# A Strassen stage with 16-bit sums and a weight scale made on chip

The Strassen-like stage of a transformer layer formed its weight and activation sums in 32 bits (the type float32r). The change forms them in float16, after scaling the weights by a power of two that the kernel takes from their L1 norm (the sum of their absolute values), and scales the results back.

## The chip, the cores and the metric

Each run uses one core of a Trainium2 chip (trn2). The metric is the device time of one execution in microseconds (us); each kernel was run several times, beside runs of the kernel before on the same chip. The experiments went in three batches, on different chips; the kernel before took 803.37, 803.18 and 803.22 us there (medians), so times are compared across batches. "Clock" is the mean granted TensorE clock of a run, 1.0 being full speed. All runs told of here were fast (within 1.5% of the fastest of their kernel). Engines: PE is TensorE's matmuls, PEld its weight loads, DVE VectorE, ACT ScalarE, POOL GpSimd.

## The reference

```python
x = A_x                                       # 2048 x 1024, bf16
h = x + attention(layernorm(x), wqkv, wo)     # 32 heads, 8 dilated keys per position
y = layernorm(h)
out = h + ((y @ w_gate) * (y @ w_up)) @ w_down   # w_gate, w_up: 1024 x 3584
```

## The kernel before

The 2048 rows go in four chunks of 512. Chunks 0 and 1 take the gate and up matmuls plainly (`ffn1`). Chunks 2 and 3 are taken together: with weights cut into halves and the two chunks as the other pair of halves, seven half-size products stand for eight (a Strassen form). There are 14 blocks (`pair_block`), each of 7 products x 4 matmuls x 2 (gate, up) = 56 matmuls of 512 columns. The weight sums are made by GpSimd, the activation sums once by VectorE. Line numbers in profiles of other kernels differ: L622 (matmul of a product) is L653 in the changed one.

```python
    def ffn1(c, lnT):
        hT = []
        for b in range(7):
            if b == 5 and c + 1 < NCH:
                hss[c + 1] = load_x(c + 1, "h", nc.sync)
            for j in range(4):
                pg = psum.tile([128, TC], F32, tag="mm", name=f"pg{c}_{b}_{j}")
                mm_group(pg, wts["wg", c, b], j, lnT)
                gs = t1k.tile([128, TC], BF, tag="t1k", name=f"gs{c}_{b}_{j}")
                nc.scalar.copy(gs[:], pg[:])
                bg.step(GROUP_US)
                pu = psum.tile([128, TC], F32, tag="mm", name=f"pu{c}_{b}_{j}")
                mm_group(pu, wts["wu", c, b], j, lnT)
                us = t1k.tile([128, TC], BF, tag="t1k", name=f"us{c}_{b}_{j}")
                nc.scalar.copy(us[:], pu[:])
                nc.vector.tensor_tensor(gs[:], gs[:], us[:], ALU.mult)
                bg.spend(0.45)
                bg.step(GROUP_US)
                hT.append(gs)
            retire(2)
        return hT

    ...
    def weight_sums(n, i):
        wt = pair["w", n]
        a11, a12 = wt[:, 0:4, i, 0:128], wt[:, 4:8, i, 0:128]
        a21, a22 = wt[:, 0:4, i, 128:256], wt[:, 4:8, i, 128:256]
        sw = wpool.tile([128, 4, 4, 128], F32R, tag="w", name=f"sw_{n}_{i}")
        nc.gpsimd.tensor_tensor(sw[:, 0], a21, a22, ALU.add)
        nc.gpsimd.tensor_tensor(sw[:, 1], sw[:, 0], a11, ALU.subtract)
        nc.gpsimd.tensor_tensor(sw[:, 2], a11, a21, ALU.subtract)
        nc.gpsimd.tensor_tensor(sw[:, 3], a12, sw[:, 1], ALU.subtract)
        pair["s", n, i] = sw
        state["live"] += 1

    def activation_sums(l2, l3):
        b11, b12, b21, b22 = l2[:, 0:4, :], l3[:, 0:4, :], l2[:, 4:8, :], l3[:, 4:8, :]
        t1 = att.tile([128, 4, TC], F32R, tag="kD", name="t1p")
        t2 = att.tile([128, 4, TC], F32R, tag="vD", name="t2p")
        t3 = att.tile([128, 4, TC], F32R, tag="prod", name="t3p")

        t4 = lnTp.tile([128, 4, TC], F16, tag="lnT", name="t4p")
        bc = att.tile([128, 4, TC], F32R, tag="oD", name="bcp")
        nc.scalar.copy(bc[:], b22)
        nc.vector.tensor_tensor(t1[:], b12, b11, ALU.subtract)
        nc.vector.tensor_tensor(t2[:], b22, t1[:], ALU.subtract)
        nc.vector.tensor_tensor(t3[:], b22, b12, ALU.subtract)
        nc.vector.tensor_tensor(t4[:], b21, t2[:], ALU.subtract)
        pair["b"] = (b11, b21, t1, t2, t3, t4, bc)

    def product(ps, lhs, rhs, fresh):
        for ko in range(4):
            nc.tensor.matmul(ps[:], lhsT=lhs[:, ko, :], rhs=rhs[:, ko, :], start=(fresh and ko == 0),
                             stop=(ko == 3), skip_group_check=not fresh)

    def pair_block(n, hts):
        b11, b21, t1, t2, t3, t4, bc = pair["b"]
        wt = pair["w", n]
        gu = range(2)
        sw = [pair["s", n, i] for i in gu]
        out = [hts, [t1k.tile([128, TC], BF, tag="t1k", name=f"up{n}_{k}")[:] for k in range(4)]]

        def bank(k, i):
            return psum.tile([128, TC], F32, tag="mm", name=f"p{k}{n}_{i}")

        xb, yb, zb, vb, p5 = [[None] * 2 for _ in range(5)]
        for i in gu:
            xb[i] = bank("x", i)
            product(xb[i], wt[:, 0:4, i, 0:128], b11, True)
            yb[i] = bank("y", i)
            nc.scalar.copy(yb[i][:], xb[i][:])
        for i in gu:
            vb[i] = bank("v", i)
            product(vb[i], sw[i][:, 0], t1, True)
            p5[i] = att.tile([128, TC], F32, tag=("lg", "t3")[i], name=f"p5{n}_{i}")
            nc.scalar.copy(p5[i][:], vb[i][:])
            product(yb[i], sw[i][:, 1], t2, False)
            zb[i] = bank("z", i)
            nc.scalar.copy(zb[i][:], yb[i][:])
        for i in gu:
            product(zb[i], sw[i][:, 2], t3, False)
            nc.vector.tensor_tensor(out[i][3], zb[i][:], p5[i][:], ALU.add)
            product(xb[i], wt[:, 4:8, i, 0:128], b21, False)
            nc.scalar.copy(out[i][0], xb[i][:])
        for i in gu:
            product(zb[i], wt[:, 4:8, i, 128:256], t4, False)
            nc.scalar.copy(out[i][2], zb[i][:])
            product(yb[i], sw[i][:, 3], bc, False)
            nc.vector.tensor_tensor(out[i][1], yb[i][:], p5[i][:], ALU.add)
        for k in (3, 0, 2, 1):
            nc.vector.tensor_tensor(out[0][k], out[0][k], out[1][k], ALU.mult)
        state["live"] -= 3

    ...
    hT = ffn1(1, lnT2)            # then, in order:
    bg.finish(atts[2])
    l2, hs2 = wo_ln2(2)           # output projection of chunk 2, layernorm
    ffn2(1, 0, hT, hs)
    bg.finish(atts[3])
    l3, hs3 = wo_ln2(3)
    activation_sums(l2, l3)
    load_pair(0); load_pair(1)
    weight_sums(0, 0)
    ffn2(1, 1, hT, hs, {0: lambda: weight_sums(0, 1)})
    ...                           # h23: where the products of gate and up go
    for n in range(NP):           # NP = 14
        if n + 1 < NP:
            weight_sums(n + 1, 0)
            weight_sums(n + 1, 1)
            if n + 2 < NP:
                load_pair(n + 2)
        ...
        pair_block(n, h23[4 * n:4 * n + 4])
    ...                           # ffn2 of chunks 2 and 3
```

`bg.step` puts pieces of the attention of later chunks, nearly all of it VectorE work, between the matmul groups.

Of the kernel before, what the change touches and what calls it, by code (L numbers as in the profile page):

```python
# [7 lines left out]

BF = mybir.dt.bfloat16
F32 = mybir.dt.float32  # L10
F32R = mybir.dt.float32r
F16 = mybir.dt.float16
ALU = mybir.AluOpType
ACTF = mybir.ActivationFunctionType
# [4 lines left out]
D = 1024  # L19
# [6 lines left out]
TC = 512  # L26
NCH = S // TC
SUB = TC // 4
KO = D // 128
# [49 lines left out]
def kernel(  # L79
# [11 lines left out]
    nc = tc.nc  # L91
# [6 lines left out]
    const = ctx.enter_context(tc.tile_pool(name="const", bufs=1))  # L98
    wpool = ctx.enter_context(tc.tile_pool(name="wstream", bufs=7))
    lnTp = ctx.enter_context(tc.tile_pool(name="lnT", bufs=3))  # L100
    lnp = ctx.enter_context(tc.tile_pool(name="ln", bufs=4))
    hp = ctx.enter_context(tc.tile_pool(name="hp", bufs=8))
    t1k = ctx.enter_context(tc.tile_pool(name="t1k", bufs=30))
    small = ctx.enter_context(tc.tile_pool(name="small", bufs=4))
    att = ctx.enter_context(tc.tile_pool(name="att", bufs=1))
    psum = ctx.enter_context(tc.tile_pool(name="psum", bufs=8, space=PSUM))
# [48 lines left out]
    wts = {}  # L155
    state = {"next": 0, "live": 0, "limit": 1}
# [343 lines left out]
    def wo_ln2(c):  # L500
# [25 lines left out]
        retire(2)  # L526
        return lnT, hs

    def ffn1(c, lnT):
        hT = []  # L530
        for b in range(7):
# [10 lines that stand above are left out]
                us = t1k.tile([128, TC], BF, tag="t1k", name=f"us{c}_{b}_{j}")  # L542
                nc.scalar.copy(us[:], pu[:])  # L543
                nc.vector.tensor_tensor(gs[:], gs[:], us[:], ALU.mult)
                bg.spend(0.45)
                bg.step(GROUP_US)
                hT.append(gs)
            retire(2)
        return hT
# [6 lines left out]
    def ffn2(c, hf, hT, hs, between={}):  # L556
        if c == NCH - 1 and hf == 1:
            for t, lo, n in ((0, 0, 512), (1, 0, 512), (2, 0, 512), (3, 0, 256), (3, 256, 256)):
                acc = psum.tile([128, n], F32, tag="mm", name=f"accl{t}_{lo}")
                for f in range(NF):  # L560
                    nc.tensor.matmul(acc[:], lhsT=hT[f][:, bass.ts(t, 128)],  # L561
                                     rhs=wts["wd", c, hf, f // 7][:, f % 7, bass.ds(lo, n)],
                                     start=(f == 0), stop=(f == NF - 1))
                ffn2_store(c, t, hf, acc, hs, lo, n)
            return
        acc = [psum.tile([128, 512], F32, tag="mm", name=f"acc{c}_{hf}_{t}") for t in range(4)]
        for b in range(4):
            for j in range(7):
                f = b * 7 + j
                for t in range(4):  # L570
                    nc.tensor.matmul(acc[t][:], lhsT=hT[f][:, bass.ts(t, 128)],  # L571
                                     rhs=wts["wd", c, hf, b][:, j, :],
                                     start=(f == 0), stop=(f == NF - 1))
                bg.step(0.86)
            retire()
            if b in between:
                between[b]()
        for t in range(4):
            ffn2_store(c, t, hf, acc[t], hs)
            bg.spend(0.7)  # L580
# [3 lines left out]
    pair = {}  # L584
# [5 lines left out]
        pair["w", n] = wt  # L590
        state["live"] += 1

    def weight_sums(n, i):
        wt = pair["w", n]
        a11, a12 = wt[:, 0:4, i, 0:128], wt[:, 4:8, i, 0:128]
        a21, a22 = wt[:, 0:4, i, 128:256], wt[:, 4:8, i, 128:256]
        sw = wpool.tile([128, 4, 4, 128], F32R, tag="w", name=f"sw_{n}_{i}")
        nc.gpsimd.tensor_tensor(sw[:, 0], a21, a22, ALU.add)  # L598
        nc.gpsimd.tensor_tensor(sw[:, 1], sw[:, 0], a11, ALU.subtract)
        nc.gpsimd.tensor_tensor(sw[:, 2], a11, a21, ALU.subtract)  # L600
        nc.gpsimd.tensor_tensor(sw[:, 3], a12, sw[:, 1], ALU.subtract)
        pair["s", n, i] = sw
        state["live"] += 1

    def activation_sums(l2, l3):
        b11, b12, b21, b22 = l2[:, 0:4, :], l3[:, 0:4, :], l2[:, 4:8, :], l3[:, 4:8, :]
        t1 = att.tile([128, 4, TC], F32R, tag="kD", name="t1p")
        t2 = att.tile([128, 4, TC], F32R, tag="vD", name="t2p")
        t3 = att.tile([128, 4, TC], F32R, tag="prod", name="t3p")

        t4 = lnTp.tile([128, 4, TC], F16, tag="lnT", name="t4p")
        bc = att.tile([128, 4, TC], F32R, tag="oD", name="bcp")
        nc.scalar.copy(bc[:], b22)
        nc.vector.tensor_tensor(t1[:], b12, b11, ALU.subtract)
        nc.vector.tensor_tensor(t2[:], b22, t1[:], ALU.subtract)
        nc.vector.tensor_tensor(t3[:], b22, b12, ALU.subtract)
        nc.vector.tensor_tensor(t4[:], b21, t2[:], ALU.subtract)
        pair["b"] = (b11, b21, t1, t2, t3, t4, bc)

    def product(ps, lhs, rhs, fresh):  # L620
        for ko in range(4):
            nc.tensor.matmul(ps[:], lhsT=lhs[:, ko, :], rhs=rhs[:, ko, :], start=(fresh and ko == 0),  # L622
                             stop=(ko == 3), skip_group_check=not fresh)

    def pair_block(n, hts):
        b11, b21, t1, t2, t3, t4, bc = pair["b"]
        wt = pair["w", n]
        gu = range(2)
        sw = [pair["s", n, i] for i in gu]
        out = [hts, [t1k.tile([128, TC], BF, tag="t1k", name=f"up{n}_{k}")[:] for k in range(4)]]  # L630

        def bank(k, i):
# [7 lines that stand above are left out]
            nc.scalar.copy(yb[i][:], xb[i][:])  # L640
        for i in gu:
            vb[i] = bank("v", i)
            product(vb[i], sw[i][:, 0], t1, True)
            p5[i] = att.tile([128, TC], F32, tag=("lg", "t3")[i], name=f"p5{n}_{i}")
            nc.scalar.copy(p5[i][:], vb[i][:])
            product(yb[i], sw[i][:, 1], t2, False)
            zb[i] = bank("z", i)
            nc.scalar.copy(zb[i][:], yb[i][:])
        for i in gu:
            product(zb[i], sw[i][:, 2], t3, False)  # L650
            nc.vector.tensor_tensor(out[i][3], zb[i][:], p5[i][:], ALU.add)
            product(xb[i], wt[:, 4:8, i, 0:128], b21, False)
            nc.scalar.copy(out[i][0], xb[i][:])  # L653
        for i in gu:
            product(zb[i], wt[:, 4:8, i, 128:256], t4, False)
            nc.scalar.copy(out[i][2], zb[i][:])
            product(yb[i], sw[i][:, 3], bc, False)
            nc.vector.tensor_tensor(out[i][1], yb[i][:], p5[i][:], ALU.add)
        for k in (3, 0, 2, 1):
            nc.vector.tensor_tensor(out[0][k], out[0][k], out[1][k], ALU.mult)  # L660
        state["live"] -= 3

    atts = {}

# [30 lines left out]
    lnT2, hs = nxt  # L695
# [4 lines left out]
        ffn2(0, hf, hT, hs)  # L700
    lnT2, hs = nxt
    hT = ffn1(1, lnT2)
    bg.finish(atts[2])
    l2, hs2 = wo_ln2(2)
    h3 = att.tile([128, 4, D], BF, tag="qD", name="h3")
# [5 lines left out]
    activation_sums(l2, l3)  # L711
    load_pair(0)
    load_pair(1)
    weight_sums(0, 0)
    ffn2(1, 1, hT, hs, {0: lambda: weight_sums(0, 1)})

    h23 = [t1k.tile([128, TC], BF, tag="t1k", name=f"hq{i}")[:] for i in range(24)]
    for i in range(4):
        ht = hp.tile([128, D], BF, tag="h", name=f"hq_h{i}")
        h23 += [ht[:, 0:TC], ht[:, TC:2 * TC]]  # L720
    for ht in (att.tile([128, KO, TC], BF, tag="oT", name="hq_o"),
               l3):
        h23 += [ht[:, k, :] for k in range(KO)]
    for i in range(4):
        ht = lnp.tile([128, D], BF, tag="ln", name=f"hq_n{i}")
        h23 += [ht[:, 0:TC], ht[:, TC:2 * TC]]
    for n in range(NP):
        if n + 1 < NP:
            weight_sums(n + 1, 0)
            weight_sums(n + 1, 1)  # L730
            if n + 2 < NP:
                load_pair(n + 2)
        else:
            state["limit"] = len(stream)
            pump()
        pair_block(n, h23[4 * n:4 * n + 4])
# [35 lines left out]
```

## Time and profile before

| | before |
|---|---|
| time, median of the first 3 runs | 803.0 us (802.61 to 803.44) |
| span of the profiled run | 801.5 us |
| start of output projection, chunk 1 | 288.56 us |
| first Strassen block | 523.39 us |
| end of the 14th block | 701.45 us, so 12.72 us each |
| TensorE busy / VectorE / ScalarE / GpSimd | 99 / 70 / 30 / 21% of the span |

Read it from TensorE: it is busy from its first microseconds to the end, so the sum of its instruction spacings is the time. The other engines matter only when they make it wait. The lines are in the prediction below.

### The profile page before, as it was taken

The page shows a single profiled execution, that of the slowest core. Times are in us where ns is not written, and L with a number is a line of the kernel's source. Part 1 is how long each engine was busy: PE and PEld are TensorE (multiplying, and loading weights), DVE is VectorE, ACT ScalarE, POOL GpSimd, SP SyncE. Part 2 cuts the span into 40 slices and gives each one's busy share as a digit, 9 for nine tenths or more (in the row PEclk, how much of TensorE's full clock was granted, in tenths as well). Part 3 has the DMA queues.
Part 4 walks back from the last instruction along what each step waited for, and adds up shares of the span by engine and source line. Part 5 has one row for each costly group of instructions (what it writes and reads, how often), then busy time and mean ns, then how long its engine had stood idle before and what let it go on. Part 6 is the DMA issues. An engine that isn't in the chain of part 4 may idle for free.

```text
span 801.5 us, 9971 instructions
## 1 busy us (share of the span) xinstructions
PE 796.4 (99%) x3801; PEld 400.9 (50%) x3801; DVE 561.3 (70%) x584; ACT 240.5 (30%) x538; POOL 164.7 (21%) x160
## 2 busy tenths in 40 slices
PE   9999999999999999999999999999999999999998
PEld 6544444444444444444444444466666666644445
DVE  6629999999899998998989917545656666311111
ACT  4626444313433311013333200144444444400000
POOL 0000000200001100001000010597878778100000
PEclk9999999999999999999999999999999999999999
DMA  7998783987954978668546695541323233476500
GB/s 263 257 237 201 175 264 97 293 242 205 338 193 160 329 233 232 194 230 262 164 128 221 176 279 148 125 130 54 105 55 104 81 78 98 143 232 194 174 27 27
DMA packets 190976, 143.27 MB, mean 179 GB/s; under 512 B 79184, under 2 KB 183760, under 8 KB 188880
## 3 DMA queue, kind: packets, MB, share of 16 engines
q1 hardware_dynamic: 187344, 120.61, 53.1%
q0 software_dynamic: 3584, 22.02, 7.9%
q8 instruction: 30, 0.49, 0.3%
q14 instruction: 18, 0.15, 0.1%
HBM read 114.29 MB, written 22.02 MB: 170 GB/s over the span
## 4 chain that ended last, share of the span: by engine, by line
PE 98%; DMA 1%; SPq 0%; DVE 0%; issue 0%
PE acc L571 21%; PE ps L392 20%; PE pg L392 12%; PE pu L392 12%; PE wo L513 7%; PE py L622 7%; PE pz L622 6%; PE px L622 6%; PE pv L622 3%; PE accl L561 3%; PE ps L354 1%; DMA w_qkv<-in_A_wqkv_dram 1%; PE ptb L235 0%; PE pt L344 0%; SPq L270 0%; SPq L273 0%
## 5 line engine op out<-in xcount | busy, mean ns | idle before, releaser
L392 PE MATMUL ps<-lnT,w_qkv 128*128 128x512 bf16 x736 | 159.7, 379 | 0.0
L392 PEld LDWEIGHTS <-w_qkv 128*128 128x128 bf16 x736 | 71.8, 98 | 85.9
L392 PE MATMUL pg<-lnT,w_wg 128*128 128x512 bf16 x448 | 105.8, 379 | 0.0
L392 PE MATMUL pu<-lnT,w_wu 128*128 128x512 bf16 x448 | 105.8, 379 | 0.0
L571 PE MATMUL acc<-w_wd,gs 128*128 128x512 bf16 x448 | 97.2, 379 | 0.0
L553 DVE TENSOR_TENSOR h<-acc,h 128x512 bf16<-128x512 f32 x28 | 17.4, 683 | 91.1 <-PE acc L571 91.1
L475 DVE TENSOR_TENSOR pv<-vD,at 128x4096 bf16<-128x4096 bf16 x32 | 72.5, 2287 | 0.3
L432 DVE TENSOR_TENSOR prod<-qD,kD 128x4096 bf16<-128x4096 bf16 x32 | 72.4, 2284 | 0.1
L303 ACT CAST sg<-ps 128x512 bf16<-128x512 f32 x96 | 54.8, 590 | 53.8 <-PE ps L392 51.8
L392 PEld LDWEIGHTS <-w_wg 128*128 128x128 bf16 x448 | 43.8, 98 | 52.9
L571 PEld LDWEIGHTS <-gs 128*128 128x128 bf16 x448 | 43.8, 98 | 52.9
L392 PEld LDWEIGHTS <-w_wu 128*128 128x128 bf16 x448 | 43.8, 98 | 52.9
L538 ACT CAST gs<-pg 128x512 bf16<-128x512 f32 x56 | 33.0, 589 | 97.8 <-PE pg L392 97.8
L513 PE MATMUL wo<-w_wo,oT 128*128 128x512 bf16 x256 | 55.9, 379 | 0.0
L622 PE MATMUL px<-lnT,w_pair 128*128 128x512 bf16 x224 | 55.6, 381 | 0.0
L487 POOL DMA_DIRECT2D od<-oD x4 | 2.2, 542 | 247.8 <-DVE oD L485 247.8
L598 POOL TENSOR_TENSOR sw<-w_pair 128x512 fp32r<-128x512 bf16 x28 | 36.2, 1293 | 76.5 <-DMA w_pair<-in_B_w_gate_dram 43.6
L543 ACT CAST us<-pu 128x512 bf16<-128x512 f32 x56 | 32.9, 588 | 55.6 <-PE pu L392 54.4
L622 PEld LDWEIGHTS <-w_pair 128*128 128x128 bf16 x336 | 28.5, 98 | 41.7 <-issue 15.2
L513 PEld LDWEIGHTS <-oT 128*128 128x128 bf16 x256 | 25.1, 98 | 30.2
L182 ACT ACTIVATE rs<-mv,eps 128x1 f32<-128x1 f32 x32 | 9.5, 296 | 101.6 <-DVE mv L179 98.0
L434 DVE TENSOR_TENSOR prod<-prod 128x4096 bf16<-128x4096 bf16 x16 | 36.6, 2288 | 0.3
(129 smaller groups left out, 1059.2 us busy)
## 6 DMA issues: line engine op xcount, KB each, us to landing
w_wd<-in_B_w_down_dram SPq DMA_DIRECT2D x32, 896.0 KB, 6.7
w_wg<-in_B_w_gate_dram SPq DMA_DIRECT2D x14, 1024.0 KB, 7.1
w_wu<-in_B_w_up_dram SPq DMA_DIRECT2D x14, 1024.0 KB, 5.4
w_wo<-in_A_wo_dram SPq DMA_DIRECT2D x8, 1024.0 KB, 7.4
w_pair<-in_B_w_gate_dram SPq DMA_DIRECT2D x14, 512.0 KB, 4.0
w_pair<-in_B_w_up_dram SPq DMA_DIRECT2D x14, 512.0 KB, 5.3
w_qkv<-in_A_wqkv_dram SPq DMA_DIRECT2D x5, 1024.0 KB, 9.3
kd<-sg SPq DMA_DIRECT2D x32, 144.0 KB, 2.9
```

What stands on the lines that cost most here:

```text
L303: nc.scalar.copy(sg[:, HB:HB + TC], ps[:])
L392: nc.tensor.matmul(ps[:], lhsT=wt[:, ko, bass.ts(j, 128)], rhs=rhs[:, ko, :], start=(ko == 0), stop=(ko == KO - 1))
L432: nc.vector.tensor_tensor(prod[:, j], qD[:], kD[:, :, o:o + SUB], ALU.mult)
L434: nc.vector.tensor_tensor(prod[:, :, 0:16], prod[:, :, 0:16], prod[:, :, 16:32], ALU.add)
L475: nc.vector.tensor_tensor(pv[:, j], vD[:, :, o:o + SUB], at[:, w, None, :].to_broadcast((128, DH, SUB)), ALU.mult)
L513: nc.tensor.matmul(ps[:], lhsT=oTs[c][:, kk, t, :], rhs=wts["wo", c, hf][:, kk, :], start=(kk == 0), stop=(kk == KO - 1))
L538: nc.scalar.copy(gs[:], pg[:])
L543: nc.scalar.copy(us[:], pu[:])
L561: nc.tensor.matmul(acc[:], lhsT=hT[f][:, bass.ts(t, 128)], rhs=wts["wd", c, hf, f // 7][:, f % 7, bass.ds(lo, n)], start=(f == 0), stop=(f ...
L571: nc.tensor.matmul(acc[t][:], lhsT=hT[f][:, bass.ts(t, 128)], rhs=wts["wd", c, hf, b][:, j, :], start=(f == 0), stop=(f == NF - 1))
L598: nc.gpsimd.tensor_tensor(sw[:, 0], a21, a22, ALU.add)
L622: nc.tensor.matmul(ps[:], lhsT=lhs[:, ko, :], rhs=rhs[:, ko, :], start=(fresh and ko == 0), stop=(ko == 3), skip_group_check=not fresh)
```

## The change

Intent: matmuls with 32-bit sums are slower than those with 16 bits (0.234 us each against 0.216 in the trace of before); the weights are scaled first so that the sums stay in float16's range, a precaution. The power of two comes from the exponent of the L1 norm of both weight matrices, summed by ScalarE while `ffn1` has the weights in SBUF anyway. The diff, cut to its core (cuts marked "...", some with a remark):

```diff
+    def abs_sum(c, b, j):                 # after each gate/up pair in ffn1
+        ...
+        nc.scalar.activation(junk[:], wt[:, bass.ts(j, 2), :], ACTF.Abs, accum_out=l1[:, k:k + 1])
+
+    def make_scale():
+        row = small.tile([128, 1], F32, tag="l1row")
+        nc.vector.tensor_reduce(row[:], l1[:], mybir.AxisListType.X, ALU.add)
+        rowb = small.tile([128, 1], BF, tag="l1rowb")
+        nc.vector.tensor_copy(rowb[:], row[:])
+        ps = psum.tile([128, TC], F32, tag="mm", name="l1ps")
+        nc.tensor.matmul(ps[:], lhsT=ones[:], rhs=rowb[:].to_broadcast((128, TC)), start=True, stop=True)
+        tot = const.tile([128, 1], F32)
+        nc.vector.tensor_copy(tot[:], ps[:, 0:1])
+        ...                               # four small VectorE operations on the exponent bits
     def ffn1(c, lnT):
...
                 nc.vector.tensor_tensor(gs[:], gs[:], us[:], ALU.mult)
+                abs_sum(c, b, j)
                 bg.spend(0.45)
...
-    def weight_sums(n, i):
...
-        sw = wpool.tile([128, 4, 4, 128], F32R, tag="w", name=f"sw_{n}_{i}")
+    def weight_sums(n):
+        raw = pair["w", n]
+        wt = wpool.tile([128, KO, 2, 256], F16, tag="w", name=f"ws_{n}")
+        nc.vector.tensor_scalar(wt[:], raw[:], scale["s"], None, ALU.mult)
+        sw = wpool.tile([128, 2, 4, 4, 128], F16, tag="w", name=f"sw_{n}")
...                                        # the same 8 GpSimd sums per block, from wt
     def activation_sums(l2, l3):
...                                        # t1..t4 in F16; the F32R copy of b22 is gone
-            nc.scalar.copy(p5[i][:], vb[i][:])
+            nc.scalar.activation(p5[i][:], vb[i][:], ACTF.Copy, scale=inv)
...                                        # and so for out[0], out[2]
-            nc.vector.tensor_tensor(out[i][3], zb[i][:], p5[i][:], ALU.add)
+            nc.vector.scalar_tensor_tensor(out[i][3], zb[i][:], inv, p5[i][:], ALU.mult, ALU.add)
...                                        # and so for out[1]
     hT = ffn1(1, lnT2)
+    make_scale()
     bg.finish(atts[2])
     l2, hs2 = wo_ln2(2)
```

More of the change, by code (lines that the diff above doesn't have):

```diff
@@ L10 @@
 F32 = mybir.dt.float32
-F32R = mybir.dt.float32r
+I32 = mybir.dt.int32
 F16 = mybir.dt.float16
@@ L527, in wo_ln2 @@
         return lnT, hs
+    l1 = const.tile([128, 56], F32)
+    ones = const.tile([128, 128], BF)
+    nc.vector.memset(ones[:], 1.0)
+    scale = {}
+    def abs_sum(c, b, j):
+        k = 28 * c + 4 * b + j
+        wt = wts["wg" if c == 0 else "wu", c, b]
+        junk = lnp.tile([128, 2, 512], BF, tag="ln", name=f"junk{c}_{b}_{j}")
+        nc.scalar.activation(junk[:], wt[:, bass.ts(j, 2), :], ACTF.Abs, accum_out=l1[:, k:k + 1])
[8 more added lines that the diff above has]
+        nc.vector.tensor_copy(tot[:], ps[:, 0:1])
+        eb = const.tile([128, 1], I32)
+        nc.vector.tensor_scalar(eb[:], tot[:].bitcast(I32), 0x7F800000, None, ALU.bitwise_and)
+        nc.vector.tensor_scalar(eb[:], eb[:], float(27 << 23), None, ALU.max)
+        sb = const.tile([128, 1], I32)
+        nc.vector.tensor_scalar(sb[:], eb[:], -1.0, float(266 << 23), ALU.mult, ALU.add)
+        ib = const.tile([128, 1], I32)
+        nc.vector.tensor_scalar(ib[:], eb[:], float(12 << 23), None, ALU.subtract)
+        scale["s"], scale["inv"] = sb[:].bitcast(F32), ib[:].bitcast(F32)
     def ffn1(c, lnT):
@@ L591, in load_pair @@
         state["live"] += 1
-    def weight_sums(n, i):
-        wt = pair["w", n]
-        a11, a12 = wt[:, 0:4, i, 0:128], wt[:, 4:8, i, 0:128]
-        a21, a22 = wt[:, 0:4, i, 128:256], wt[:, 4:8, i, 128:256]
-        sw = wpool.tile([128, 4, 4, 128], F32R, tag="w", name=f"sw_{n}_{i}")
-        nc.gpsimd.tensor_tensor(sw[:, 0], a21, a22, ALU.add)
-        nc.gpsimd.tensor_tensor(sw[:, 1], sw[:, 0], a11, ALU.subtract)
-        nc.gpsimd.tensor_tensor(sw[:, 2], a11, a21, ALU.subtract)
-        nc.gpsimd.tensor_tensor(sw[:, 3], a12, sw[:, 1], ALU.subtract)
-        pair["s", n, i] = sw
+    def weight_sums(n):
[3 more added lines that the diff above has]
+        sw = wpool.tile([128, 2, 4, 4, 128], F16, tag="w", name=f"sw_{n}")
+        for i in range(2):
+            a11, a12 = wt[:, 0:4, i, 0:128], wt[:, 4:8, i, 0:128]
+            a21, a22 = wt[:, 0:4, i, 128:256], wt[:, 4:8, i, 128:256]
+            nc.gpsimd.tensor_tensor(sw[:, i, 0], a21, a22, ALU.add)
+            nc.gpsimd.tensor_tensor(sw[:, i, 1], sw[:, i, 0], a11, ALU.subtract)
+            nc.gpsimd.tensor_tensor(sw[:, i, 2], a11, a21, ALU.subtract)
+            nc.gpsimd.tensor_tensor(sw[:, i, 3], a12, sw[:, i, 1], ALU.subtract)
+        pair["a", n], pair["s", n] = wt, sw
         state["live"] += 1
@@ L606, in activation_sums @@
         b11, b12, b21, b22 = l2[:, 0:4, :], l3[:, 0:4, :], l2[:, 4:8, :], l3[:, 4:8, :]
-        t1 = att.tile([128, 4, TC], F32R, tag="kD", name="t1p")
-        t2 = att.tile([128, 4, TC], F32R, tag="vD", name="t2p")
-        t3 = att.tile([128, 4, TC], F32R, tag="prod", name="t3p")
-        t4 = lnTp.tile([128, 4, TC], F16, tag="lnT", name="t4p")
-        bc = att.tile([128, 4, TC], F32R, tag="oD", name="bcp")
-        nc.scalar.copy(bc[:], b22)
-        nc.vector.tensor_tensor(t1[:], b12, b11, ALU.subtract)
-        nc.vector.tensor_tensor(t2[:], b22, t1[:], ALU.subtract)
-        nc.vector.tensor_tensor(t3[:], b22, b12, ALU.subtract)
-        nc.vector.tensor_tensor(t4[:], b21, t2[:], ALU.subtract)
-        pair["b"] = (b11, b21, t1, t2, t3, t4, bc)
+        t12 = att.tile([128, 2, 4, TC], F16, tag="kD", name="t12p")
+        t34 = att.tile([128, 2, 4, TC], F16, tag="vD", name="t34p")
+        t1, t2, t3, t4 = t12[:, 0], t12[:, 1], t34[:, 0], t34[:, 1]
+        nc.vector.tensor_tensor(t1, b12, b11, ALU.subtract)
+        nc.vector.tensor_tensor(t2, b22, t1, ALU.subtract)
+        nc.vector.tensor_tensor(t3, b22, b12, ALU.subtract)
+        nc.vector.tensor_tensor(t4, b21, t2, ALU.subtract)
+        pair["b"] = (b11, b21, t1, t2, t3, t4, b22)
     def product(ps, lhs, rhs, fresh):
@@ L625, in pair_block @@
     def pair_block(n, hts):
-        b11, b21, t1, t2, t3, t4, bc = pair["b"]
-        wt = pair["w", n]
+        b11, b21, t1, t2, t3, t4, b22 = pair["b"]
+        wt, sw, inv = pair["a", n], pair["s", n], scale["inv"]
         gu = range(2)
-        sw = [pair["s", n, i] for i in gu]
         out = [hts, [t1k.tile([128, TC], BF, tag="t1k", name=f"up{n}_{k}")[:] for k in range(4)]]
@@ L642, in pair_block @@
             vb[i] = bank("v", i)
-            product(vb[i], sw[i][:, 0], t1, True)
+            product(vb[i], sw[:, i, 0], t1, True)
             p5[i] = att.tile([128, TC], F32, tag=("lg", "t3")[i], name=f"p5{n}_{i}")
-            nc.scalar.copy(p5[i][:], vb[i][:])
-            product(yb[i], sw[i][:, 1], t2, False)
+            nc.scalar.activation(p5[i][:], vb[i][:], ACTF.Copy, scale=inv)
+            product(yb[i], sw[:, i, 1], t2, False)
             zb[i] = bank("z", i)
@@ L649, in pair_block @@
         for i in gu:
-            product(zb[i], sw[i][:, 2], t3, False)
-            nc.vector.tensor_tensor(out[i][3], zb[i][:], p5[i][:], ALU.add)
+            product(zb[i], sw[:, i, 2], t3, False)
+            nc.vector.scalar_tensor_tensor(out[i][3], zb[i][:], inv, p5[i][:], ALU.mult, ALU.add)
             product(xb[i], wt[:, 4:8, i, 0:128], b21, False)
-            nc.scalar.copy(out[i][0], xb[i][:])
+            nc.scalar.activation(out[i][0], xb[i][:], ACTF.Copy, scale=inv)
         for i in gu:
             product(zb[i], wt[:, 4:8, i, 128:256], t4, False)
-            nc.scalar.copy(out[i][2], zb[i][:])
-            product(yb[i], sw[i][:, 3], bc, False)
-            nc.vector.tensor_tensor(out[i][1], yb[i][:], p5[i][:], ALU.add)
+            nc.scalar.activation(out[i][2], zb[i][:], ACTF.Copy, scale=inv)
+            product(yb[i], sw[:, i, 3], b22, False)
+            nc.vector.scalar_tensor_tensor(out[i][1], yb[i][:], inv, p5[i][:], ALU.mult, ALU.add)
         for k in (3, 0, 2, 1):
             nc.vector.tensor_tensor(out[0][k], out[0][k], out[1][k], ALU.mult)
-        state["live"] -= 3
+        state["live"] -= 2
     atts = {}
@@ L713, with first_sums @@
     load_pair(1)
-    weight_sums(0, 0)
-    ffn2(1, 1, hT, hs, {0: lambda: weight_sums(0, 1)})
+    def first_sums():
+        weight_sums(0)
+    ffn2(1, 1, hT, hs, {0: first_sums})
     h23 = [t1k.tile([128, TC], BF, tag="t1k", name=f"hq{i}")[:] for i in range(24)]
@@ L721 @@
     for ht in (att.tile([128, KO, TC], BF, tag="oT", name="hq_o"),
-               l3):
+               lnTp.tile([128, KO, TC], BF, tag="lnT", name="hq_l"),
+               att.tile([128, 2 * KO, TC], BF, tag="prod", name="hq_p")):
         h23 += [ht[:, k, :] for k in range(KO)]
-    for i in range(4):
-        ht = lnp.tile([128, D], BF, tag="ln", name=f"hq_n{i}")
-        h23 += [ht[:, 0:TC], ht[:, TC:2 * TC]]
     for n in range(NP):
         if n + 1 < NP:
-            weight_sums(n + 1, 0)
-            weight_sums(n + 1, 1)
+            weight_sums(n + 1)
             if n + 2 < NP:
```

## The prediction

The forecast's sum came to 798.6 us (803.0 - 8.8 + 4.4) and its point to 799.1. The 1.3 us in the plan of the weight scaling was the estimate for one scaling; the changed kernel took 1.280 us for it (L627). Its activation sums, put at about 1.2 us, took 1.22 to 1.23 (L645 to L648). The 0.09 us for a pointer scale is an estimate too, near the 0.09 to 0.10 us between the Ln and the Exp of the trace (295 and 203 ns, medians of L182 and L183); measured were 687 ns against 586.

> **What bounds the kernel now.** I read the busy shares first, then the chain that ended last, then the groups of the Strassen stage with shapes kept apart, then the timeline around the place where the scale is to be made. The page's busy line and its chain:
>
> ```profile
> PE 796.4 (99%) x3801; PEld 400.9 (50%) x3801; DVE 561.3 (70%) x584; ACT 240.5 (30%) x538; POOL 164.7 (21%) x160
> PE 98%; DMA 1%; SPq 0%; DVE 0%; issue 0%
> ```
>
> TensorE is never idle after its start and carries 98% of the chain. Only its own pace, or a new hole in it, can move the time. So the pace is the next view: the chain in order of time, in which every link is TensorE, one line for a run of matmuls (start us, us, name, count).
>
> ```profile
> 445.69 1.73 PE pu L392 x8
> 447.42 13.81 PE wo L513 x64
> ...
> 536.09 1.74 PE px L622 x8
> 537.84 0.94 PE pv L622 x4
> ...
> 548.81 1.74 PE px L622 x8
> ...
> 701.45 72.53 PE acc L571 x336
> ```
>
> A bf16 matmul of 512 columns is spaced 13.81/64 = 0.2158 us. A product with 32-bit sums is 0.94 us for 4, 0.234 each. A Strassen block runs from one px run to the next, 548.81 - 536.09 = 12.72 us; the 14 blocks lie between 523.39 and 701.45, also 12.72 each. The groups by shape (from 540 us on) show which operations are slow (count, total us, mean ns, idle before):
>
> ```profile
> L622 PE MATMUL px<-lnT,w_pair 128*128 128x512 bf16 x200 | 49.7, 381 | 0.0
> L622 PE MATMUL py<-bcp,sw 128*128 128x512 f32 x104 | 33.5, 444 | 0.0
> L622 PE MATMUL pz<-t4p,w_pair 128*128 128x512 f16 x104 | 26.8, 380 | 0.0
> L622 PEld LDWEIGHTS <-w_pair 128*128 128x128 bf16 x304 | 25.7, 98 | 37.8 <-issue 14.1
> L622 PEld LDWEIGHTS pz<-t3p,sw 128*128 128x128 f32 x104 | 19.6, 188 | 5.4
> L660 DVE TENSOR_TENSOR hq<-hq,up 128x512 bf16<-128x512 bf16 x22 | 29.4, 1394 | 0.0
> L660 DVE TENSOR_TENSOR hq_n<-hq_n,up 128x512 bf16<-128x512 bf16 x8 | 2.8, 419 | 0.0
> ```
>
> Of the 56 matmuls of a block, 32 (v, y twice, first z; each for gate and up) have 32-bit operands, and their weight loads take 188 ns against 98. The float16 sum t4 against bf16 weights already runs at 380 ns, as the bf16 px does, so 16 bits of either kind, mixed too, should have the quick pace. The last two rows are one VectorE operation: 1394 ns while GpSimd is summing weights, 419 ns in the last blocks, where it no longer is.
>
> [...] Here the softmax exponential over 1024 took 1056 ns[...], and the Ln with a bias pointer 296 ns against 200 for the Exp without.
>
> **The change part by part.**
> *Matmuls.* 32 slow ones per block become quick: a block is then 56 x 0.2158 = 12.09 us. Gain (12.72 - 12.09) x 14 = **8.8 us**, all on the chain.
>
> *The L1 norm on ScalarE.* 56 ACTIVATEs of 1024 elements with an accumulator, estimated 1.1 to 1.25 us each (from the 1056 ns), about 65 us in the two first FFN stages, where ScalarE has two casts of 0.59 us in every 3.45 us. After us(j) it has 1.14 us free before gs(j+1), which the sum fits closely; us(j+1), which VectorE waits for, is not touched. Off the chain. The exception is behind the softmax exponential: at 405.7 us ScalarE had waited for VectorE and then had casts queued; a sum between them delays the second multiply there by about 1 us, of which later idle VectorE time (0.28 and 0.33 us) takes back some 0.6. I carry 0.5 us forward.
>
> *Making the scale.* This is the new cost. One matmul (ones x row sums) is put in TensorE's order between the first FFN of chunk 1 and the output projection of chunk 2, and waits for VectorE. The timelines there, ScalarE then VectorE:
>
> ```profile
> 447.45 0.59 ACT L543 CAST us<-pu 128x512 bf16<-128x512 f32 x1 [1.14 <-PE pu L392]
> ```
> ```profile
> 448.07 0.42 DVE L544 TENSOR_TENSOR gs<-gs,us 128x512 bf16<-128x512 bf16 x1 [0.33 <-ACT us L543]
> 448.41 2.28 DVE L485 TENSOR_TENSOR oD<-oD,pv 128x4096 bf16<-128x4096 bf16 x1
> 450.62 1.28 DVE L515 TENSOR_TENSOR h<-wo,h 128x512 bf16<-128x512 f32 x2
> ```
>
> TensorE starts wo at 447.42. ScalarE's last sum would end near 449.1. But VectorE first has the multiply and the last attention addition, to 450.7, as both are ahead of the new reduce in program order (+0.5 from above: 451.2). Then the reduce over 56 elements (estimate 0.22 us, like the 0.21 us aggregate), the cast to bf16 (0.15), a semaphore (0.05): the matmul starts near 451.6 and wo 0.22 us later, at 451.8. That is **4.4 us** of TensorE idle or on the extra matmul. Nothing later absorbs it, for TensorE has no slack. The five small VectorE operations on the exponent run beside wo.
>
> *Scaling back.* Two fp32 copies and four casts per block get a pointer scale: 6 x 0.09 = 0.5 us more of ScalarE, 5.8 to about 6.4 of 12.09 us. Each still ends inside the product that separates it from its reader. The four PSUM additions on VectorE gain a scalar multiply and stay near 0.7 us. No cost on the chain.
>
> *Weight scaling on VectorE.* One tensor_scalar over 4096 elements per block, 16 bits in and out[...]. After a block ends, VectorE has the last addition (to 0.76 us), four multiplies, then this; the next thing TensorE needs of it is the first z addition, ready at 6.05 us and to be done by 8.64 us, when z is written again. GpSimd's 8 sums (1.16 us each, undisturbed, in the trace: 9.3 us) now start after the scaling. With multiplies at 0.42 the scaling ends at 0.76 + 1.7 + 1.3 = 3.8 us, GpSimd ends at 13.1, which is 1.0 in the next block, so at most the first multiply meets it. A steady state: the scaled weights at 4, the sums at 13.3 at the latest, and their first reader at 13.8 needs only the first of them, done at 5.2. So the multiplies should fall from 1394 to around 500 to 600 ns, worth nothing in time.
>
> *Activation sums.* In 16 bits the four VectorE operations fall from 2.29 to 3.24 us each to about 1.2; the ScalarE copy (1.90 us) goes. They ended at 516.8, TensorE needs them at 525: worth nothing.
>
> *Buffers.* Still three 8 KB tiles per block in seven; the raw weights are now freed early. Five instead of four down-projection tiles may be prefetched at the end. No wait expected either way.
>
> Sum: 803.0 - 8.8 + 4.4 = 798.6.
>
> **The rivals.** (a) *The hole lets the clock fall.* [...] (b) *VectorE or GpSimd becomes the bound of a block.* [...] If GpSimd took 1.5 us on float16, 12 us of sums per 12.09 us period would leave no room. Against it: [...]GpSimd took 1.15 to 1.16 us whether its operands were bf16 or fp32. (c) *ScalarE's sums fill PSUM.* At 204 us ScalarE had waited 10 us for VectorE with casts queued. I played the queue through with a sum after each pair: it works off a pair in about 2.2 us while TensorE makes one in 3.45, and the bank for each new group is free at least 1.3 us early. No loss; had it, 1 to 3 us, 800 to 802. (d) *The hole is smaller*, if VectorE's last attention addition comes later in its order than I read: 1.9 us after 447.4 at the least, 796. (e) *The 32-bit pace is not what makes the block long*, so no gain and only the hole: 807. The spacing of 0.234 against 0.216 in this trace speaks against it.
>
> **Range and chances.** [...] Down to 796 if the hole is halved, up to 804 with the clock and some waits in the blocks: eight times in ten. Faster by 2% (below 787) needs a gain more than the matmuls hold: 0.02. Slower by 2% (above 819) needs rival (b): 0.05.
>
> **What would show it.** Right: blocks of 12.1 us, no 188 ns weight loads, one TensorE hole near 447 us of 4 to 4.5 us ended by VectorE, multiplies near 0.5 us, scaling near 1.3 us, the projection and down-projection stages unchanged. Wrong: blocks longer than 12.2 us with TensorE waiting for VectorE or GpSimd; a hole outside 3 to 6 us; matmuls behind the hole at half pace; holes in the first FFN stages.

## The result

The changed kernel took 800.48 us (median of 4 runs, 799.69 to 800.83) against 803.22 us (4 runs) for the kernel before: ratio 0.9964, 95% interval 0.9947 to 0.9982. Ratios here are the mean time of one kernel's fast runs over that of the other's of the same rounds, so not quite the ratio of the medians. The time lies inside the predicted range, 1.4 us above the point.

The page's busy line and chain after the change:

```profile
PE 785.1 (98%) x3732; PEld 364.7 (46%) x3802; DVE 529.2 (66%) x606; ACT 304.4 (38%) x649; POOL 150.7 (19%) x160
PE 73%; DVE 22%; issue 2%; SPq 1%; DMA 1%; ACT 1%; DVEq 0%
```

The chain looks as if VectorE had become 22% of the path. It has not: the chain is followed back from the end, crosses to VectorE at the one place where TensorE waited for it, and then runs along VectorE's backlog before that place. The list of TensorE's waits puts the size to it (who, for whom: us in total, times, longest); its other waits are under 1.5 us, all within the first 62 us:

```profile
PE l1ps L547 <- DVE rowb L545: 3.7, 1, 3.7
```

The blocks, from the chain in order of time:

```profile
614.34 1.73 PE px L653 x8
626.42 1.73 PE px L653 x8
...
698.94 4.75 PE acc L602 x22
```

A block is 12.09 us now. The groups by shape from 540 us on show why, and what became of VectorE and GpSimd:

```profile
L653 PE MATMUL pv<-t12p,sw 128*128 128x512 f16 x104 | 26.7, 379 | 0.0
L653 PEld LDWEIGHTS <-sw 128*128 128x128 f16 x420 | 41.1, 98 | 49.6
L627 DVE TENSOR_SCALAR ws<-w_pair,sb 128x4096 f16<-128x4096 bf16 x12 | 15.4, 1280 | 0.0
L690 DVE TENSOR_TENSOR hq<-hq,up 128x512 bf16<-128x512 bf16 x24 | 8.5, 418 | 0.0
L634 POOL TENSOR_TENSOR sw<-ws 128x512 f16<-128x512 f16 x25 | 28.8, 1152 | 0.0
```

Every weight load takes 98 ns; the multiplies fell from 1394 to 418 ns; GpSimd's sums took 1152 ns (1.14 to 1.17 us in the trace of before from 517.77 to 537.86 us).

The timelines around the new hole (the stretch in which TensorE idles), VectorE and then TensorE:

```profile
448.68 0.43 DVE L574 TENSOR_TENSOR gs<-gs,us 128x512 bf16<-128x512 bf16 x1
449.02 2.29 DVE L485 TENSOR_TENSOR oD<-oD,pv 128x4096 bf16<-128x4096 bf16 x1
451.22 0.20 DVE L543 TENSOR_REDUCE row<-l 128x1 f32<-128x56 f32 x1
451.46 0.16 DVE L545 CAST rowb<-row 128x1 bf16<-128x1 f32 x1
```
```profile
451.68 0.53 PE L547 MATMUL l1ps<-rowb,ones 128*128 128x512 bf16 x1 [3.65 <-DVE rowb L545]
452.00 14.27 PE L513 MATMUL wo<-w_wo,oT 128*128 128x512 bf16 x57
```

And the busy time in stretches (stretch, length, busy us and instructions of PE, PEld, DVE, ACT, POOL; then the granted clock, DMA share, GB/s):

```profile
448.00:451.80 3.80, 0.15 (x2) 0.12 (x2) 3.59 (x5) 1.63 (x3) 0.20 (x1) 1.00 0.84 269
451.80:455.20 3.40, 3.40 (x9) 1.22 (x9) 0.68 (x5) 0.00 (x0) 0.36 (x1) 0.50 1.07 398
455.20:458.60 3.40, 3.40 (x17) 1.50 (x16) 2.04 (x4) 0.00 (x0) 0.00 (x0) 1.00 0.37 157
```

TensorE idles, and then gets half its clock (0.50) for 3.4 us: 9 matmuls against 17 in the next stretch of the same length, so about 1.7 us lost. Busy shares don't show this; the clock column and the count do. In the table below a tenth or two of it falls on the ones matmul, so in the row before that of the projection.

The balance of the two traces, each row from the same starts in both:

| stretch | before | after | difference |
|---|---|---|---|
| to the projection of chunk 1 | 288.56 | 289.17 | +0.61 |
| from there to the last `ffn1` group of chunk 1 (445.53, 446.14) | 156.97 | 156.97 | 0 |
| from that to the projection of chunk 2 (447.25, 452.00) | 1.72 | 5.86 | +4.14 |
| from that to the first block (523.39, 529.73) | 76.14 | 77.73 | +1.59 |
| 14 blocks (to 701.45, 698.94) | 178.06 | 169.21 | -8.85 |
| to the end (801.5, 798.9) | 100.05 | 99.96 | -0.09 |
| sum | 801.5 | 798.9 | -2.6 |

A wait in the profile is shorter than what it costs: it is counted from the end of the last matmul's record, which lasts 379 ns, while the next matmul could have started 216 ns after that one, so 0.16 us come on top (an estimate from these two figures). With 3.65 of wait and 0.32 for the ones matmul (451.68 to 452.00) that makes 4.13 of the 4.14 us. The 0.61 us come from the first weights landing 0.22 us later and from a wait of 0.24 us (0.40 with the 0.16) for ScalarE at 61 us. Two of the experiments below that keep this part of the program (e1, e4) have no such wait at 61 us, so I take it for scatter between runs.

### The profile page after: what moved, and what is told of

Same layout as the page of the kernel before. It is cut to its first block, busy times and chain, and to the rows that moved or that the text cites. A ratio compares the mean times of both kernels' runs of the same rounds, so it can differ in the third digit from the quotient of the medians.

```text
span 798.9 us, 9984 instructions
## 1 busy us (share of the span) xinstructions
PE 785.1 (98%) x3732; PEld 364.7 (46%) x3802; DVE 529.2 (66%) x606; ACT 304.4 (38%) x649; POOL 150.7 (19%) x160
## 4 chain that ended last, share of the span: by engine, by line
PE 73%; DVE 22%; issue 2%; SPq 1%; DMA 1%; ACT 1%; DVEq 0%
PE acc L602 21%; PE pg L392 9%; PE pu L392 9%; PE pz L653 6%; PE py L653 6%; PE px L653 6%; PE wo L513 5%; DVE pv L475 4%; DVE prod L432 4%; PE ps L392 3%; PE accl L592 3%; PE pv L653 3%; DVE prod L434 2%; DVE oD L485 2%; DVE pv L483 2%
## 5 line engine op out<-in xcount | busy, mean ns | idle before, releaser
L653 PEld LDWEIGHTS <-sw 128*128 128x128 f16 x448 | 43.8, 98 | 52.9
L653 PE MATMUL px<-lnT,ws 128*128 128x512 bf16 x211 | 52.6, 379 | 0.6
L653 PEld LDWEIGHTS <-ws 128*128 128x128 f16 x336 | 32.9, 98 | 39.6
L182 ACT ACTIVATE rs<-mv,eps 128x1 f32<-128x1 f32 x32 | 9.5, 295 | 107.6 <-DVE mv L179 103.9
L632 POOL TENSOR_TENSOR sw<-ws 128x512 f16<-128x512 f16 x28 | 32.3, 1152 | 87.5 <-PE acc L602 46.4
```

The lines of the kernel that those rows point to most:

```text
L632: nc.gpsimd.tensor_tensor(sw[:, i, 0], a21, a22, ALU.add)
```

## The experiments

Theory: the change gains 8.85 us in the blocks and gives back some 4 us in the hole and 1.7 us in the half clock behind it; everything else is off the path. Rivals: the clock falls for another reason than idleness (the float16 work); the L1 sums cost time in `ffn1`; VectorE's or GpSimd's order in the blocks limits them.

| run | median us (runs) | ratio to before (95%) |
|---|---|---|
| the change | 800.48 (4) | 0.9964 (0.9947 to 0.9982) |
| e1_matmul_later | 794.67 (4) | 0.9891 (0.9877 to 0.9904) |
| e2_hole_filled | 798.67 (5) | 0.9941 (0.9927 to 0.9954) |
| e3_hole_shorter | 797.12 (5) | 0.9926 (0.9914 to 0.9939) |
| e4_constant_scale | 794.31 (4) | 0.9887 (0.9873 to 0.99) |
| e5_scale_only | 808.6 (4) | 1.0064 (1.0048 to 1.0079) |
| e6_hole_three | 798.74 (5) | 0.9937 (0.9925 to 0.995) |
| e7_hole_shifted | 801.59 (5) | 0.9982 (0.997 to 0.9995) |
| e8_hole_shifted_more | 802.6 (5) | 0.9993 (0.998 to 1.0005) |
| e9_one_product_fp32 | 797.31 (5) | 0.9926 (0.9914 to 0.9939) |
| e10_scaling_twice | 797.68 (4) | 0.9933 (0.9918 to 0.9948) |
| e11_scaling_four_times | 834.21 (4) | 1.0381 (1.0366 to 1.0395) |

All eleven gave a correct result.

### Taking the hole away

```diff
-    def make_scale():
+    def norm_row():                  # reduce and cast only
...
+    def make_scale():                # the ones matmul and what follows it
+        rowb = scale["rowb"]
...
     hT = ffn1(1, lnT2)
-    make_scale()
+    norm_row()
     bg.finish(atts[2])
     l2, hs2 = wo_ln2(2)
+    make_scale()
```

> The changed kernel with the ones matmul of the scale moved behind the output projection of chunk 2 (the reduce and cast stay where they are on VectorE), so TensorE no longer waits for VectorE there. Theory (hole of 3.97 us plus 1.76 us of half clock behind it): no hole, no half clock, 800.5 - 3.97 - 1.76 = 794.7 to 795 us, clock 1.00. Rival (the clock falls for another reason, such as the float16 work): 796.5 and a mean clock of 0.998 still. Rival (the blocks or the L1 sums lose elsewhere): 797 or more.

Measured 794.67 us, clock 1.0. The stretch that held the hole (columns as before):

```profile
440.00:470.00 30.00, 30.00 (x141) 13.59 (x140) 23.93 (x39) 8.07 (x19) 4.11 (x5) 1.00 0.73 177
```

TensorE is busy through, at full clock, and the float16 stage is as it was: its blocks run from 523.24 to 692.46, 12.09 us each. So the float16 work doesn't lower the clock, and hole and half clock together were worth 800.48 - 794.67 = 5.8 us. This version beats both kernels.

### Filling the hole without shortening it

```diff
+        fill = psum.tile([128, TC], F32, tag="mm", name="fill")
+        for _ in range(16):
+            nc.tensor.matmul(fill[:], lhsT=warm[:, 0:128], rhs=warm[:], start=True, stop=True)
         ps = psum.tile([128, TC], F32, tag="mm", name="l1ps")
```

> The changed kernel with 16 matmuls on zeros put in front of the ones matmul, some 3.5 us of work inside the hole. TensorE still cannot go on before VectorE is done. Theory: the hole's own 4 us stay, the half clock behind it does not come: 800.5 - 1.76 = 798.7 us, clock 1.00. Rival (the half clock is not from idleness): 800.5 and clock 0.998.

Measured 798.67 us; the clock behind the place stays at 1.00:

```profile
451.00:454.40 3.40, 3.40 (x16) 1.59 (x17) 1.37 (x6) 0.00 (x0) 0.43 (x1) 1.00 1.08 395
```

The matmuls on zeros do nothing but keep TensorE busy, and they save 1.8 us. The ones matmul and the DMA traffic (395 GB/s here, 398 in the change) are still there, so they did not lower the clock. That splits the 5.8 us: 4.0 for the hole itself (798.67 - 794.67), 1.8 for the half clock. So here the half clock followed from the idleness: it came behind 3.65 us of it in the change and did not come with the hole filled.

### The cost without the gain, and the gain without the cost

e5 adds `abs_sum`, `make_scale` and its place in the order to the kernel before, whose blocks keep their 32-bit sums; the scale is used by nobody.

```diff
+    l1 = const.tile([128, 56], F32)      # abs_sum and make_scale as in the change
...
                 nc.vector.tensor_tensor(gs[:], gs[:], us[:], ALU.mult)
+                abs_sum(c, b, j)
...
     hT = ffn1(1, lnT2)
+    make_scale()
```

> The kernel before with the L1 sums and the making of the scale added, the scale then used by nobody; the Strassen stage keeps its 32-bit sums. Theory (the cost side of the change is the hole and the half clock and nothing else): 803.2 + 4.0 + 1.76 = 809 us, clock 0.998, blocks of 12.72 us. Rival (part of the cost comes from the float16 stage): 807 or less.

Measured 808.6 us, 5.4 us above the kernel before; blocks of 12.71 us. The hole is the same 3.65 us. In its profiled run, the slowest of the four (810.67), the half clock lasted twice as long, 6.8 us; the projection of chunk 2 then took 16.55 us where 64 matmuls of 0.2158 make 13.81:

```profile
452.18 16.55 PE wo L514 x64
```

One of the four runs (808.16) had a mean clock of 1.0, so it escaped the fall, without being faster than a run at 0.998 (807.67). The early part scatters by such amounts: in the profiled runs the projection of chunk 1 starts between 287.96 (e10) and 290.52 us (e11), and the two are as far apart at the projection of chunk 0 (163.64 and 166.20), before any L1 sum. A mean clock of 0.996 in place of 0.998 fits a half clock of twice the length; four runs without a trace have it (one of the change, two of e7, one of e8).

e4 keeps the 16-bit part and drops everything that makes the scale.

```diff
-                abs_sum(c, b, j)
...
-        row = small.tile([128, 1], F32, tag="l1row")
-        ...                              # reduce, cast, ones matmul, exponent
+        sb = const.tile([128, 1], F32)
+        nc.vector.memset(sb[:], 0.5)
+        ib = const.tile([128, 1], F32)
+        nc.vector.memset(ib[:], 2.0)
+        scale["s"], scale["inv"] = sb[:], ib[:]
```

> The 16-bit part alone: no L1 sums on ScalarE, no reduce, no ones matmul; the scale and its inverse are constants written once (0.5 and 2.0), still read as per-partition operands. Result should stay right for these inputs. Theory (the sums cost nothing off the chain): the same as e1_matmul_later within 0.4 us, 794.4 to 795. Rival (the sums on ScalarE cost time in the FFN stages): 1 us or more below e1.

Measured 794.31 us, 0.36 us below e1, of which one matmul of 0.22 us is accounted for; the intervals overlap. So 56 sums on ScalarE, 71 us of its time with the reads of the accumulator (medians in the change 1.06 us each, and 0.19 us for the read), cost at most a few tenths.

### How long a hole the clock stands

e3 makes the scale ahead of VectorE's last attention addition:

```diff
                 abs_sum(c, b, j)
+                if (c, b, j) == (1, 6, 3):
+                    make_scale()
                 bg.spend(0.45)
...
     hT = ffn1(1, lnT2)
-    make_scale()
```

> The changed kernel with the whole making of the scale put ahead of VectorE's last attention addition (2.29 us). ScalarE's last sum, which ends at 449.7 us, then sets the hole: 2.0 to 2.2 us idle instead of 3.65. Theory: 800.5 - 1.6 - 1.76 = 797.1 us and clock 1.00[...]. Rival (any hole lowers the clock): 798.9 and clock 0.998. Rival (ScalarE is not the next bound): a hole below 1.5 us, under 796.5.

Measured 797.12 us. The hole is now ended by ScalarE's last sum, as expected, and is 2.16 us long. Four of the five runs have clocks of 0.999 to 1.0 and 796.52 to 797.8 us, one has 0.998 and 799.34. The profiled run had the full clock around the hole. No trace of the run at 0.998 is at hand; by its time and its mean clock it looks like a fall, behind a hole of about 2.16 us.

e6 lengthens that hole with memsets of `ones` to the value it has:

```diff
         row = small.tile([128, 1], F32, tag="l1row")
+        for _ in range(5):
+            nc.vector.memset(ones[:], 1.0)
```

> As e3_hole_shorter, with five small memsets ahead of the reduce, so that the hole is about 3.0 us instead of 2.16. Theory[...]: 797.1 + 0.85 = 798 us, all runs at clock 1.00 in this stretch. Rival[...]: about 799.7 and half clock behind the hole.

The hole became 2.57 us, not 3.0, as the memsets partly fit into VectorE's own wait for ScalarE. The runs fall into two groups: 796.98 and 797.17 us at clock 1.0, 798.74, 798.85 and 798.97 us at 0.998. The profiled run is of the second:

```profile
449.40:449.80 0.40, 0.15 (x1) 0.16 (x2) 0.16 (x1) 0.00 (x0) 0.00 (x0) 0.84 0.07 21
449.80:453.20 3.40, 3.40 (x9) 1.20 (x9) 2.80 (x6) 0.00 (x0) 0.00 (x0) 0.52 0.94 302
453.20:456.60 3.40, 3.40 (x18) 1.55 (x16) 2.15 (x5) 0.00 (x0) 0.56 (x1) 1.00 0.61 249
```

The clock falls behind 2.57 us of idleness, for the same 3.4 us, and the two groups differ by 1.8 us. My expectation of clock 1.00 in all runs is refuted.

e7 and e8 keep the long hole and move it, with 4 and 8 matmuls on zeros before it and 5 and 10 memsets before the reduce. Each expectation gave two outcomes, without a half clock (the first) and with it (the second).

```diff
+        for _ in range(5):               # e8: 10
+            nc.vector.memset(ones[:], 1.0)
...
+        fill = psum.tile([128, TC], F32, tag="mm", name="fill")
+        for _ in range(4):               # e8: 8
+            nc.tensor.matmul(fill[:], lhsT=warm[:, 0:128], rhs=warm[:], start=True, stop=True)
```

> The changed kernel with four matmuls on zeros before the hole and five memsets before the reduce: the hole is as long as in the changed kernel (about 3.65 us) and lies 0.86 us later. [...] 800.5 + 0.86 - 1.76 = 799.6 us and clock 1.00. [...] 801.3 us with half clock behind the hole in all or some runs.

> As e7_hole_shifted with eight matmuls and ten memsets: a hole of about 3.65 us, 1.7 us later[...]. [...] 800.5 + 1.7 - 1.76 = 800.4 us and clock 1.00. [...] 802.2 us and half clock in all runs.

Measured 801.59 and 802.6 us, with holes of 3.91 and 4.34 us in the profiled runs, somewhat longer than meant. All ten runs have a clock of 0.996 or 0.998: the second outcome, so moving the hole by such amounts did not avoid the fall. By the mean clock of each run (0.998 or less counted as a fall) the clock fell in 17 of 18 runs with holes of 3.65 to 4.34 us (the change 4 of 4, e5 3 of 4, e7 5 of 5, e8 5 of 5), in 3 of 5 at 2.57 us and in 1 of 5 at 2.16 us. In these runs, the longer the hole, the larger the share with a fall.

When the clock falls can be read from the traces, where short stretches of the busy-time view give the moment. The half clock began at 451.80 us in the change, 450.76 in e5, 449.67 in e6, 451.65 in e7 and 453.42 in e8: between 2.6 and 4.0 us after TensorE had gone idle, so not a fixed time after the last matmul. In the change it lasted 3.41 us (to 455.21). A stretch of that length before each start held 3.29, 2.84, 2.57, 3.41 and 3.41 us of idleness. What the hardware counts, and why the clock fell in only 3 of 5 and 1 of 5 runs behind the shorter holes, is not shown.

### Where the 32-bit cost sits

```diff
+            nc.gpsimd.tensor_tensor(s0[i][:], a21, a22, ALU.add)      # s0 and t1 in F32R
...
-            product(vb[i], sw[:, i, 0], t1, True)
+            product(vb[i], pair["s0", n][i], t1, True)
```

> e1_matmul_later with one of the seven products, v, put back to 32 bits on both sides (8 of the 56 matmuls of a block). Theory (a 32-bit matmul is spaced 0.234 instead of 0.216 us, and the gain is the number of matmuls times that): 8 x 14 x 0.0181 = 2.0 us more than e1, 796.7 us, blocks of 12.23 us. Rival (the block gets long from changing between 32 and 16 bits, not from the number of 32-bit matmuls): about as many changes remain for v as before, so half or more of the 8.85 us, 799 us. Rival (VectorE or GpSimd bound the block): nothing, 794.7.

Measured 797.31 us, 2.6 us over e1. The blocks:

```profile
524.23 1.73 PE px L660 x8
536.50 1.73 PE px L660 x8
```

12.27 us each, so 0.18 us per block and 2.5 us in 14, against 2.0 expected. Most of the cost seems to go with the number of 32-bit matmuls, and a part with the changes between the two kinds. This is an estimate, two unknowns from two kernels, and no test of its own: 32 such matmuls in 4 runs cost 0.634 us per block (before), 8 in 2 runs cost 0.181 (e9), which makes 0.017 us per matmul and 0.022 per run of them. No run has float16 weights with 32-bit activations, so whether the weight load or the moving operand sets the pace stays open.

### How much room the blocks have

```diff
-        nc.vector.tensor_scalar(wt[:], raw[:], scale["s"], None, ALU.mult)
+        for _ in range(2):               # e11: 4
+            nc.vector.tensor_scalar(wt[:], raw[:], scale["s"], None, ALU.mult)
```

> e1_matmul_later with the weight scaling on VectorE done twice (1.28 us more per block, same result). Theory (VectorE has over 2.5 us free before the z addition is due): no change, 794.7 us, blocks of 12.09 us, multiplies partly slowed by GpSimd, which now ends about 1.3 us later. Rival (VectorE's order is already tight): up to 1.3 us per block, 810 us or so.

Measured 797.68 us, 3.0 us over e1: my expectation failed. The blocks start at 12.09 us and drift to 12.54, when TensorE waits about 0.3 us for VectorE's z addition (PE waits of e10, two of four such lines; seven waits, 2.1 us in all, 3.2 with the 0.16 us that come on top of each, of the 3.4 us by which the 14 blocks are longer than those of e1):

```profile
PE pz L658 <- DVE hq_l L686: 0.6, 2, 0.3
PE pz L658 <- DVE hq_o L686: 0.6, 2, 0.3
```

The four multiplies of a block took 2.19 us, then 3.06 in the next block: a later scaling makes GpSimd's sums end later, these then run into the next block's multiplies and slow them (0.9 us of sums beside the 2.19, 2.1 us beside the 3.06), and that makes the next scaling later still (from 2.10 us after the multiplies' start to 2.99). I had counted VectorE's free time in one block and not this loop. In the changed kernel itself the loop is open by a hair (GpSimd's last sum of a block, then VectorE's four multiplies):

```profile
613.73 1.16 POOL L635 TENSOR_TENSOR sw<-ws,sw 128x512 f16<-128x512 f16 x1
```
```profile
615.04 1.42 DVE L690 TENSOR_TENSOR hq_h<-hq_h,up 128x512 bf16<-128x512 bf16 x4
```

GpSimd ends at 614.89, VectorE begins at 615.04.

> e1_matmul_later with the weight scaling done four times (3.8 us more of VectorE per block). Theory by my timing of the block: the sums on GpSimd end 4 us into the next block, so the multiplies there are slow again (1.3 us each), the scalings end near 9.6 us, the z addition comes some 1.5 to 2.4 us too late for TensorE's next product into that bank: blocks of about 14 us, 815 to 828 us. Rival (the slack is larger than I reckon): 797 or less.

Measured 834.21 us, above the range I gave. TensorE waits up to 2.9 us for the z addition, twelve times (PE waits of e11, the first two of five such lines, which sum to 26.0 us; then the first two of the twelve from TensorE's timeline):

```profile
PE pz L658 <- DVE hq L686: 11.1, 5, 2.9
PE pz L658 <- DVE hq_l L686: 4.5, 2, 2.9
```
```profile
548.52 1.81 PE L658 MATMUL pz<-t34p,ws 128*128 128x512 f16 x4 [2.24 <-DVE hq L686]
563.97 1.02 PE L658 MATMUL pz<-t34p,ws 128*128 128x512 f16 x4 [1.51 <-DVE hq L686]
```

The chain I described is there; what I left out is that such waits lower the clock as well. Waits of about 1.5 us and of 2.9 us (the first of them 2.24) take turns. Behind each of the six long ones the clock is halved, as the 1.81 us for four matmuls show against 1.02; behind the six short ones it is not. With 6 x 1.7 us for that (the loss in the change, taken over as an estimate) and 12 x 0.16 us on top, the 26.0 us become 38.1, and the 14 blocks are 38.0 us longer than in e1 (207.26 against 169.22). So rival (b) of the prediction, blocks held up by VectorE, can be brought about: one more scaling (e10) already costs 3.0 us, three more cost 39.5.

## Why the prediction was right or wrong

The forecast was right in direction and size, and in its mechanism but for one step, the clock: matmuls behind the hole at half pace, which it had named among the signs of being wrong, did come. By its steps:

- **Matmuls, -8.8 us.** Measured -8.85: blocks of 12.09 us, no 188 ns loads. Undone alone (e5 against the change) the blocks are 12.71 us again. Right.
- **L1 norm, 0.** e4 against e1: at most 0.4 us. Right. The 0.5 us that I carried forward from the softmax place was not there: the second multiply was late by 1.0 us as foreseen, but VectorE's later idle time took back all of it, and the last multiply came at 448.68, exactly 0.61 after its place before.
- **Making the scale, +4.4 us.** Measured 4.14 in the trace and 4.0 by e1 and e2; VectorE's last attention addition ends the wait, as the prediction says, and after it came 0.20 us for the reduce, 0.16 for the cast and 0.06 to the matmul's start (the prediction's semaphore). Right, less the 0.5 above. Most of that was made up, by luck, in two places: the prediction counted from 447.42 us, but the projection's first matmul starts at 447.25 before the change, and the ones matmul took 0.32 us, not 0.22.
- **The clock, rival (a).** This is the step that was mis-sized: its term added 0.5 us to the sum. What the term rested on was not shown by the trace of before. The fall came in 17 of 18 runs with such holes and cost 1.7 to 1.8 us: half the pace for 3.41 us is 1.7. It also came behind shorter holes, of 2.57 us in e6 and of 2.24 in e11. With 1.8 added to the sum of 798.6 the point becomes 800.4.
- **VectorE and GpSimd in the blocks, no wait.** Right: no TensorE wait there. The multiplies fell to 418 ns, more than the 500 to 600 predicted, for GpSimd ended 0.55 us into the block, 0.15 us before them, instead of 1.0 us into it, which is some 0.2 us after their start. But the steady state is tighter than the text lets one believe (e10).
- **Scaling back, activation sums, buffers: 0.** Right. ScalarE's scaled copies take 687 ns against 586, VectorE's fused additions 751 against 692; neither shows in TensorE's waits.
- **Rivals (c), (d), (e).** No TensorE wait in `ffn1` (c); the hole was not smaller (d); the 32-bit pace was what made the blocks long (e9), with a small part for the changes (e).

## What to carry to other kernels

On this kernel, which one engine bounds, a small serial chain that this engine had to wait for (reduce, cast, a single matmul) was paid in full, while 71 us of work on an engine with idle time cost next to nothing: issue the producer early and place the consumer one stage later in the bound engine's order, as e1 does for 5.8 us. Add to the price of a TensorE hole the chance of a half clock behind it, 1.7 to 1.8 us here (by the mean clock in 1 of 5 runs with a hole of 2.16 us, 3 of 5 at 2.57, 17 of 18 at 3.65 to 4.34). Before moving work to an engine inside a loop, follow the loop for several turns: a delay that slows its own cause can use up slack that a single turn shows as free (e10: blocks of 12.09 us that drift to 12.54).
